# Attention's end taken apart: halves, f32r parts, earlier rows, later ranking

## Chip, cores and metric

One NeuronCore of one Trainium2 chip. The metric is device microseconds of one execution; lower is better. Traced times count from the start of the profiled span. PE is the matmul engine, DVE the vector engine, ACT the scalar engine, POOL the GpSimd engine, and SP the engine that issues the plain DMAs.

## What is computed

Decayed causal attention, then two mixture-of-experts layers. Cut to what matters here:

```python
attn_out = _attn_ref(q, k, v, f)             # 2 batches, 8 heads, 576 positions, head size 64
x = attn_out.transpose(0, 2, 1, 3).reshape(1152, 512)
# layer 1: each token goes to ONE of 8 experts (argmax of x @ w_gate), capacity 288
disp[e, counts[e]] = x[i]                    # slots are given in token order
h = relu(disp @ w1[e]);  y = h @ w2[e]       # 512 -> 1024 -> 512, float32
out[i] = gate_w[i] * y[expert_idx[i], pos[i]]
# layer 2: the two best of 8 experts by noisy logits, weighted, same matrix sizes
```

## The kernel before

**Attention** (`phase_a`) works in nine units of 128 token rows (`ORDER` 0, 1, 2, 3, 4, 6, 7, 8, 9; the last is 9, called `LAST`; unit 0 holds the first rows of both batches). A unit has four head pairs, and a step of the loop over `n` takes one pair through scores, softmax, transposes and the product with V, each stage some steps behind. Work at a unit's end is entered in a table with `at(step, function, unit)`. With n the step of a unit's last product plus one:

- `fin` (line 317) copies the product from PSUM to `xT` on ACT;
- `finx` (line 333) makes, for two head pairs at a time, token rows (`xr`) and gate logits (`lgp`) with float32 matmuls on PE (line 340), which DVE scales (lines 344 and 347);
- `route1` (line 361) finds each token's expert (DVE) and the softmax weight (ACT);
- `route2` (line 389) counts tokens ahead of each token with three small matmuls (`pp`), makes the slot `sl` on DVE and starts a scatter of the rows to `xs` in HBM from POOL (line 426).

The rows of units 8 and 9 come too late to go through HBM for the first expert. `route2` therefore keeps them on chip (`g.late1`) with a one-hot matrix `oh` (line 403). `route2(8)` has SP read the first expert's 192 rows `xg0` from `xs` (line 425), ahead of the scatters of units 8 and 9. `place` (line 434) transposes `xg0` into two PSUM banks `pa` and adds unit 8 as a matmul with its one-hot; `first` (line 874) adds unit 9 (line 884) and splits the sum into f32r high and low parts `X` (lines 887 and 888). The rank of the experts by load (`rank_count`, `rank_order`, lines 675 to 700) is the last thing that attention emits; its order decides which rows and weights SP asks for next.

**Layer 1** (`moe1`): three experts run in f32r with split weights, five in float32. `Weights.split` makes `whi` on ACT (line 760) and `wlo` on DVE (line 768) of a 128x512 weight block. `ffn1(0, f)` multiplies X with block f (lines 844 and 845, three PSUM banks in turn), ACT copies half of the result (`ha`, line 848), DVE adds the other half (`hs`, line 849), ACT applies the relu (`H`, line 852). After `ffn1(0, 0)` and `ffn1(0, 1)` one more block is split, between `hs` and `H`.

**Order.** In attention SP and PE run in the order of the program and the other engines in an order that the framework plans; both layers run in the program's order on every engine. The pools `mp`, `wp` and `wr2` of the layers take the memory of attention's pool `ap`, so their first writer waits until everything that reads or writes an `ap` tile is over, a DMA that reads its slot numbers `sl` included. Two accesses to one PSUM bank of which one writes keep their order too: in `rank_order` the matmul of line 698 writes the bank that the copies of lines 696 and 697 read.

Of the kernel before, what the change touches and what calls it, by code (L numbers as in the profile page):

```python
# [134 lines left out]
def phase_a(g, q, k, v, f, wg, noise, out):  # L135
# [180 lines left out]

    def fin(i):
        b, c = units[i]
        s0, r = (0, P) if i == 0 else CHUNKS[c]
        nmax, rsum, pv = st[i]  # L320
        xT = ap.tile([P, KD, P], F32, tag="xT", name="xT", bufs=2)
        nc.scalar.activation(xT[:, :, :r], pv[:, :, :r], AF.Copy)
# [8 lines left out]
        st[i] = (xT, rinv, xr, lgp)  # L331

    def finx(i, half):
        b, c = units[i]
        s0, r = (0, P) if i == 0 else CHUNKS[c]
        xT, rinv, xr, lgp = st[i]
# [10 lines left out]
        nc.vector.tensor_tensor(  # L347
            xr[:r, h0 * D:(h0 + 4) * D].rearrange("q (j h d) -> q j h d", j=2, h=2), pxv[:, :, :P].rearrange("q j (h d) -> q j h d", h=2),
            rv[:, :, :, None].to_broadcast([r, 2, 2, D]), op=ALU.mult)

# [9 lines left out]

    def route1(i):
        b, c = units[i]
        s0, r = (0, P) if i == 0 else CHUNKS[c]
        xT, rinv, xr, lgp = st[i]
# [4 lines left out]
        lg, mx, gs, ef, lim, ng = s[:r, 0:8], s[:r, 8:16], s[:r, 16:17], s[:r, 17:18], s[:r, 18:19], s[:r, 20:21]  # L369
# [3 lines left out]
        nc.vector.max_index(iu[:r], mx, lg)  # L373
        nc.vector.tensor_copy(ef, iu[:r, 0:1])
# [14 lines left out]
    def route2(i):  # L389
# [10 lines left out]
        if i >= LAST - 1:  # L400
            oh = cp.tile([P, CAP1[0]], F32, tag=f"oh{i}", name="oh0")
            nc.vector.scalar_tensor_tensor(s[:, 22:23], pp[:, 0:1], 1.0, ohb[:, 0:1], op0=ALU.add, op1=ALU.mult)
            nc.vector.tensor_scalar(oh, g.iow[:, :CAP1[0]], s[:, 22:23], None, op0=ALU.is_equal)
            g.late1.append((xr, oh))
        nc.vector.scalar_tensor_tensor(s[m, 32:40], pp[m, :E], 1.0, ohb[m], op0=ALU.mult, op1=ALU.mult, accum_out=pos)
# [27 lines left out]
    def place(h):  # L433
# [4 lines left out]
        for d in (2 * h, 2 * h + 1):  # L438
            for t in range(2):
                nc.tensor.matmul(g.pa1[h][:, d % 2, t * T:(t + 1) * T], g.xg0[:T, t, d * P:(d + 1) * P], g.ident[:T, :T], start=d % 2 == 0 and t == 0, stop=False)  # L440
# [43 lines left out]
    at(first[6] - 8, load_v, 5)  # L484
    for i in ORDER:
        n = last[i] + LAG + 1
        at(n, fin, i)
        n2 = n + 1 if i == LAST else n + 2
        at(n + 1, finx, i, 0)
        at(n2, finx, i, 1)  # L490
        at(n2, route1, i)
        if i == LAST:
            at(n + 1, place, 0)
            at(n + 3, place, 1)
        at(max(n + (2 if i == LAST else 3), 21 + i if i else 0), route2, i)
    at(last[4] + LAG + 5, route2, 5)
    for n in range(len(work) + LAG + 9):
# [23 lines left out]
        if n >= 20:  # L521
            init_step(g, g.init2)
    g.order1.rank(ohs, g.caps[:, 0:E], g.pxx)

# [142 lines left out]
class Order:  # L667
    def __init__(self, g, name):
        self.g, self.name, self.reg, self.perm = g, name, {}, None

    def rank(self, ohs, caps, pool):
        self.rank_count(ohs, pool)
        self.rank_order(caps, pool)

# [112 lines left out]
def moe1(g, x_rows, w1, w2, wg2, wn2):  # L787
# [87 lines left out]
    def first():  # L875
# [4 lines left out]
        X[0] = mp.tile([P, KD, 2 * C], F32R, tag="X", name="X", bufs=1)  # L880
        xr, oh = g.late1[1]
        for d in range(KD):
            pa = g.pa1[d // 2]
            nc.tensor.matmul(pa[:, d % 2, :], xr[:, d * P:(d + 1) * P], oh, start=False, stop=d % 2 == 1)
            if d % 2:
# [361 lines left out]
```

## Time and profile before

| what | us |
|---|---|
| median of 3 runs (lowest, highest) | 572.6 (571.42, 573.81) |
| the profiled execution | 571.73 |
| its span in the trace | 569.9 |
| PE busy in the span | 548.5 |
| DVE busy | 330.8 |
| ACT busy | 257.0 |
| POOL busy | 108.6 |

Times of single instructions come from the profiled execution. Around its span lie 1.8 us; its own time is 0.9 us under the median of the runs. The trace says for each stretch what ran on each engine, what an engine waited for, and the share of full speed that was granted to PE's clock.

### The profile page before, as it was taken

The page shows a single profiled execution, that of the slowest core. Times are in us where ns is not written, and L with a number is a line of the kernel's source. Part 1 is how long each engine was busy: PE and PEld are TensorE (multiplying, and loading weights), DVE is VectorE, ACT ScalarE, POOL GpSimd, SP SyncE. Part 2 cuts the span into 40 slices and gives each one's busy share as a digit, 9 for nine tenths or more (in the row PEclk, how much of TensorE's full clock was granted, in tenths as well). Part 3 has the DMA queues.
Part 4 walks back from the last instruction along what each step waited for, and adds up shares of the span by engine and source line. Part 5 has one row for each costly group of instructions (what it writes and reads, how often), then busy time and mean ns, then how long its engine had stood idle before and what let it go on. Part 6 is the DMA issues. An engine that isn't in the chain of part 4 may idle for free.

```text
span 569.9 us, 11856 instructions
## 1 busy us (share of the span) xinstructions
PE 548.5 (96%) x4288; PEld 505.5 (89%) x4288; DVE 330.8 (58%) x1100; ACT 257.0 (45%) x642; POOL 108.6 (19%) x168
## 2 busy tenths in 40 slices
PE   8999999999999999999998999999999999999994
PEld 4566776677899999999998999999999999999993
DVE  4577767776754542332335765756666666766642
ACT  3656555553556442122125344444454545454520
POOL 4010003100000302202201720130313121224131
PEclk9999999999999999999999999999999999999998
DMA  6988917925499968678777279967586667642021
GB/s 149 241 209 223 290 57 230 374 88 198 112 369 315 319 241 263 215 233 276 239 243 208 69 213 370 288 211 205 177 221 196 218 192 230 192 121 59 23 71 49
DMA packets 103858, 116.80 MB, mean 205 GB/s; under 512 B 38189, under 2 KB 73037, under 8 KB 103792
## 3 DMA queue, kind: packets, MB, share of 16 engines
q1 hardware_dynamic: 97120, 99.86, 59.4%
q0 software_dynamic: 6528, 16.06, 8.3%
q8 instruction: 36, 0.59, 0.5%
q14 instruction: 30, 0.25, 0.1%
q10 hardware_dynamic: 144, 0.04, 0.0%
HBM read 91.63 MB, written 25.85 MB: 206 GB/s over the span
## 4 chain that ended last, share of the span: by engine, by line
PE 81%; DVE 5%; issue 4%; DMA 4%; ACT 3%; SPq 2%; POOL 0%; POOLq 0%; ACTq 0%; DVEq 0%
PE py L1020 19%; PE ps L1009 19%; PE py L858 14%; PE psn L834 7%; PE ps L844 3%; PE pyr L581 3%; PE sc L248 2%; PE pyr L1042 2%; PE pv L315 2%; PE pt L289 2%; DMA kn<-in_k_dram 2%; PE ps L845 1%; PE pt L206 1%; PE pt L978 1%; DVE t L258 1%
## 5 line engine op out<-in xcount | busy, mean ns | idle before, releaser
L768 DVE TENSOR_TENSOR wlo<-wr,whi 128x512 fp32r<-128x512 f32 x152 | 102.9, 689 | 25.4 <-ACT whi L760 22.9
L1009 PE MATMUL ps<-X,whi 128*128 128x312 f32 (+4 forms) x512 | 110.2, 306 | 0.0
L1020 PE MATMUL py<-H,whi 128*128 128x312 f32 (+4 forms) x512 | 109.8, 306 | 0.0
L760 ACT ACTIVATE whi<-wr 128x512 fp32r<-128x512 f32 x152 | 93.0, 625 | 27.5 <-PE py L1020 21.3
L1009 PEld LDWEIGHTS ps<-X,whi 128*128 128x128 f32 x512 | 83.4, 189 | 0.1
L1020 PEld LDWEIGHTS py<-H,whi 128*128 128x128 f32 x512 | 83.4, 188 | 0.0
L858 PE MATMUL py<-H,wr 128*128 128x192 f32 (+7 forms) x512 | 80.9, 314 | 0.0
L1009 PE MATMUL ps<-X,wlo 128*128 128x312 f32 (+4 forms) x256 | 77.4, 302 | 0.0
L1020 PE MATMUL py<-H,wlo 128*128 128x312 f32 (+4 forms) x256 | 77.3, 302 | 0.0
L858 PEld LDWEIGHTS py<-H,wr 128*128 128x128 f32 x512 | 76.0, 190 | 0.8
L638 POOL DMA_INDIRECT x<-yr,sl x30 | 34.4, 1146 | 134.2 <-ACT Xn L820 48.8
L266 ACT ACTIVATE pr<-t,nmax 128x192 f32<-128x192 f32 (+4 forms) x72 | 41.9, 583 | 37.5 <-DVE nmax L258 31.5
L1045 POOL DMA_INDIRECT out_dram<-ot,tk x24 | 27.4, 1140 | 148.2 <-DVE ot L1044 147.8
L1011 ACT ACTIVATE H<-ps 128x312 fp32r<-128x312 f32 (+4 forms) x64 | 27.1, 424 | 61.2 <-PE ps L1009 59.0
L1013 DVE SCALAR_TENSOR_TENSOR H<-ps,H 128x312 fp32r<-128x312 f32 (+4 forms) x64 | 30.4, 474 | 31.3 <-ACT H L1011 30.8
L1009 PEld LDWEIGHTS ps<-X,wlo 128*128 128x128 f32 x256 | 48.2, 188 | 0.0
L1020 PEld LDWEIGHTS py<-H,wlo 128*128 128x128 f32 x256 | 48.1, 188 | 0.0
L834 PE MATMUL psn<-Xn,wr 128*128 128x176 f32 (+4 forms) x320 | 46.3, 295 | 0.0
L834 PEld LDWEIGHTS psn<-Xn,wr 128*128 128x128 f32 x320 | 43.5, 190 | 0.0
L258 DVE CUSTOM_DVE_ANT_0 t<-sc,WB 128x192 f32<-128x192 f32 (+3 forms) x64 | 28.6, 477 | 5.4 <-PE sc L251 3.7
L844 PE MATMUL ps<-X,whi 128*128 128x384 f32 (+2 forms) x96 | 31.4, 383 | 0.3 <-DVE hs L849 0.2
L248 PE MATMUL sc<-kT,qT 64*128 64x288 f32 (+4 forms) x264 | 30.1, 330 | 0.4 <-DVE nmax L258 0.3
(261 smaller groups left out, 805.6 us busy)
## 6 DMA issues: line engine op xcount, KB each, us to landing
wr<-in_moe_w_dram SPq DMA_DIRECT2D x128, 512.0 KB
xs<-z SPq DMA_DIRECT2D x18, 264.0 KB
x<-z SPq DMA_DIRECT2D x16, 258.0 KB
WB<-ncum SPq DMA_DIRECT2D x4, 576.0 KB
out_dram<-z SPq DMA_DIRECT2D x9, 256.0 KB
qn<-in_q_dram SPq DMA_DIRECT2D x8, 256.0 KB
kn<-in_k_dram SPq DMA_DIRECT2D x8, 256.0 KB
x2g<-x SPq DMA_DIRECT2D x3, 628.9 KB
```

Of the source, the lines that this page charges most:

```text
L248: nc.tensor.matmul(ps[hh][:r, :a1 - a0], a[sl, p, :r], bb[sl] if i == 0 else bb[sl, a0:a1], start=m == 0, stop=m == 2 and (i == 0 or a1 < w))
L258: nc.vector.tensor_tensor_reduce(out=ts[hh][:r, a0:a1], in0=ps[hh][:r, :a1 - a0], in1=WB[b][:r, h, a0:a1] if i else Wd[0][:r, h, :r], op0= ...
L266: nc.scalar.activation(dst, src, AF.Exp, bias=nmax[:r, h:h + 1], scale=-1.0, accum_out=rsum[:r, h:h + 1])
L638: d = nc.gpsimd.indirect_dma_start(out=g.x2, out_offset=bass.IndirectOffsetOnAxis(ap=sl[:T, t, kk:kk + 1], axis=0), in_=yr[:T, t], in_offs ...
L760: self.g.nc.scalar.activation(self.hi[u], self.g.stream.view(self.base + u), AF.Copy)
L768: self.g.nc.vector.tensor_tensor(self.lo[u], self.g.stream.view(self.base + u), self.hi[u], op=ALU.subtract)
L834: nc.tensor.matmul(ps[:, :C], w[:, d, :], X[e][:, d, :], start=d == 0, stop=d == KD - 1)
L844: nc.tensor.matmul(ps[:, :2 * C], hi[:, d, :], X[e][:, d, :], start=d == 0, stop=False)
L858: nc.tensor.matmul(py[dd][:, :C], w[:, dd, :], H[e][:, f, :], start=f == 0, stop=f == KF - 1)
L1009: nc.tensor.matmul(ps[:, :C], w[:, d, :], X[e][:, x, d, :], start=d == 0 and i == 0, stop=d == KD - 1 and i == 2)
L1013: nc.vector.scalar_tensor_tensor(H[e][:, 1, f, :], ps[:, :C], 0.0, H[e][:, 0, f, :], op0=ALU.max, op1=ALU.subtract)
L1020: nc.tensor.matmul(py[dd][:, :C], w[:, dd, :], H[e][:, x, f, :], start=f == 0 and i == 0, stop=f == KF - 1 and i == 2)
```

## The change

1. **Last unit in halves.** `fin(9)` is two ACT copies. The first half's copy and `finx(9, 0)` move ahead of the last head pair's product; the second half's `finx` follows `place(0)`. The rows of its second half are scaled by four ACT copies in place of one DVE instruction.
2. **f32r parts.** A new `halves` copies the rows of units 8 and 9 to an f32r high part on ACT and subtracts it on DVE for a low part, 256 columns at a time. The one-hots become f32r, and `place8` and `first` multiply both parts.
3. **First expert's rows.** `early_rows` requests `xg0` in two DMAs three steps before the last unit's end, and `place` no longer holds unit 8. `xg0` and unit 8's parts lie in `ap` slots of the loaded K and Q rows.
4. **Routing in two pieces.** `route1` becomes `route1a` (maximum and its index) and `route1b` (the rest). For units before 8 `route1a` moves one step later, `route1b` two, `route2` two. For unit 8 nothing moves, for unit 9 all follow `place8(1)`.
5. **Ranking.** `rank` at attention's end goes. `rank_count` stands among the first weight splits, `rank_order` after `ffn1(0, 1)`, and with it the requests for the next experts' rows and weights. The two weight blocks that the first expert still lacks are requested before it (limit 8).
6. The slot numbers of unit 8 move from `ap` to the pool that stays (`cp`), as those of unit 9 did.

```diff
-    def fin(i):
+    def fin(i, half=None):
...
+        ps = slice(0, KD) if half is None else slice(2 * half, 2 * half + 2)
+        if half == 1:
+            nc.scalar.activation(st[i, "x"][0][:, ps, :r], pv[:, ps, :r], AF.Copy)
+            return
...
+    def halves(i, half):
+        x = g.late1[i]
...
+        m = slice(256 * half, 256 * half + 256)
+        nc.scalar.activation(x[1][:, m], x[0][:, m], AF.Copy)
+        nc.vector.tensor_tensor(x[2][:, m], x[0][:, m], x[1][:, m], op=ALU.subtract)
...
+        if i == LAST and half == 1:
+            for h in range(4):
+                nc.scalar.activation(xr[:, (h0 + h) * D:(h0 + h + 1) * D], pxv[:, h // 2, h % 2 * D:h % 2 * D + D], AF.Copy, scale=rinv[:, h0 + h:h0 + h + 1])
...
+        if i >= LAST - 1:
+            if half == 0:
+                g.late1.append([xr])
+            if i < LAST or half == 0:
+                halves(i - LAST + 1, half)
...
+        if i == LAST:
+            halves(1, 1)
...
-            oh = cp.tile([P, CAP1[0]], F32, tag=f"oh{i}", name="oh0")
+            oh = cp.tile([P, CAP1[0]], F32R, tag=f"oh{i}", name="oh0")
...
-        elif i == LAST:
-            sl = cp.tile([P, 1], I32, tag="sll", name="sl")
+        elif i >= LAST - 1:
+            sl = cp.tile([P, 1], I32, tag=f"sl{i}", name="sl")
...
-        if i == LAST - 1:
-            g.xg0 = cp.tile([P, 2, DM], F32, tag="xg0", name="xg0")
-            T = CAP1[0] // 2
-            nc.sync.dma_start(g.xg0[:T], g.xs[0:2 * T, :DM].rearrange("(t p) w -> p t w", p=T))
...
+    def early_rows():
+        T = CAP1[0] // 2
+        g.xg0 = [ap.tile([P, DM], F32, tag=t, name="xg0", bufs=2) for t in ("kn", "qn")]
+        for t in range(2):
+            nc.sync.dma_start(g.xg0[t][:T], g.xs[t * T:(t + 1) * T, :DM])
...
-        xr, oh = g.late1[0]
+
+    def place8(h):
+        _, hi, lo, oh = g.late1[0]
         for d in (2 * h, 2 * h + 1):
-            nc.tensor.matmul(g.pa1[h][:, d % 2, :], xr[:, d * P:(d + 1) * P], oh, start=False, stop=False)
+            for x in (hi, lo):
+                nc.tensor.matmul(g.pa1[h][:, d % 2, :], x[:, d * P:(d + 1) * P], oh, start=False, stop=False)
...
+    for i in ORDER[:-1]:
         n = last[i] + LAG + 1
+        m = n + 2 if i == LAST - 1 else n + 3
         at(n, fin, i)
...
+        at(n + 2, finx, i, 1)
+        at(m, route1a, i)
+        at(m if i == LAST - 1 else m + 1, route1b, i)
+        at(max(n + 3 if i == LAST - 1 else n + 5, 21 + i if i else 0), route2, i)
+    n = last[LAST] + LAG + 1
+    at(n - 3, early_rows)
+    at(n - 2, fin, LAST, 0)
+    at(n - 1, finx, LAST, 0)
+    at(n, fin, LAST, 1)
+    at(n, place, 0)
+    at(n + 1, finx, LAST, 1)
+    for fn, a in ((place8, (0,)), (place, (1,)), (place8, (1,)), (route1a, (LAST,)), (route1b, (LAST,)), (route2, (LAST,))):
+        at(n + 1, fn, *a)
...
-    g.order1.rank(ohs, g.caps[:, 0:E], g.pxx)
...
     W.split()
     first()
-    xg[1] = rows(1)
-    xg[2] = rows(2)
-    g.stream.limit = 9 * E
+    g.stream.limit = 8
     g.stream.pump()
-    W.split(5)
+    W.split(2)
+    g.order1.rank_count(g.ohs, g.pxx)
+    W.split(3)
...
             ffn1(e, f)
+            if e == 0 and f == 1:
+                g.order1.rank_order(g.caps[:, 0:E], g.pxx)
+                xg[1] = rows(1)
+                xg[2] = rows(2)
+                g.stream.limit = 9 * E
+                g.stream.pump()
```

## Rows read from the trace of the kernel before

Lengths and starts are in us.

**Rows 1.** The page, part 4: shares of the chain that ended last.

```profile
PE 81%; DVE 5%; issue 4%; DMA 4%; ACT 3%; SPq 2%; POOL 0%; POOLq 0%; ACTq 0%; DVEq 0%
```

**Rows 2.** Stretches: length, busy time (instructions) of PE, PEld, DVE, ACT, POOL; clock, DMA.

```profile
130.00:140.00 10.00, 9.28 (x110) 7.51 (x109) 5.52 (x29) 4.13 (x11) 0.97 (x1) 1.00 0.67 233
160.00:170.00 10.00, 10.00 (x65) 9.86 (x64) 6.57 (x12) 5.86 (x12) 0.00 (x0) 1.00 1.07 367
```

**Rows 3.** Timeline of PE, 139 to 158: start, length, line, tiles, count.

```profile
139.74 1.25 PE L340 MATMUL px<-IW,xT 128*128 128x144 f32 x8 [0.72 <-ACT xT L322]
140.82 1.03 PE L440 MATMUL pa<-ident,xg 96*128 96x96 f32 x8
141.69 0.84 PE L443 MATMUL pa<-oh,xrl 128*128 128x192 f32 x4
144.57 1.24 PE L884 MATMUL pa<-oh,xrl 128*128 128x192 f32 x6
147.48 0.42 PE L844 MATMUL ps<-X,whi 128*128 128x384 f32 x1
150.40 0.36 PE L844 MATMUL ps<-X,whi 128*128 128x384 f32 x1
150.69 0.36 PE L844 MATMUL ps<-X,whi 128*128 128x384 f32 x1
151.64 0.44 PE L844 MATMUL ps<-X,whi 128*128 128x384 f32 x1 [0.22 <-DVE hs L849]
157.45 1.48 PE L858 MATMUL py<-H,wr 128*128 128x192 f32 x8
```

**Rows 4.** Timeline of DVE, 143 to 153, columns as before.

```profile
143.12 0.32 DVE L403 TENSOR_SCALAR oh<-iow,rtl 128x192 f32<-128x192 f32 x1
145.45 0.15 DVE L682 SCALAR_TENSOR_TENSOR rks<-prk,tie 8x8 f32<-8x8 f32 x1
145.96 0.21 DVE L686 SCALAR_TENSOR_TENSOR rks<-io,rks,one 8x8 f32<-8x8 f32 x1
146.81 0.55 DVE L888 TENSOR_TENSOR X<-pa,X 128x384 fp32r<-128x384 f32 x1
147.69 0.56 DVE L888 TENSOR_TENSOR X<-pa,X 128x384 fp32r<-128x384 f32 x1
151.23 0.35 DVE L849 TENSOR_TENSOR hs<-ps,ha 128x192 f32<-128x192 f32 x1
152.75 0.69 DVE L768 TENSOR_TENSOR wlo<-wr,whi 128x512 fp32r<-128x512 f32 x1 [0.16 <-ACT whi L760]
```

**Rows 5.** Source line L760, 142.75 to 142.85: ACT's sequencer.

```profile
L760 ACTq EVENT_SEMAPHORE  x1: 1112/1112/1112, 142.7 to 142.7; - x1
```

**Rows 6.** Timeline of POOL, the scatter of unit 8.

```profile
138.82 0.97 POOL L426 DMA_INDIRECT xs<-xrl,sl  x1 [12.31 <-DMA x<-z]
```

**Rows 7.** Timeline of PE in the second layer's first expert.

```profile
331.21 0.38 PE L698 MATMUL prq<-rks 8*128 8x8 f32 x2 [0.87 <-DVE perm L697]
```

**Rows 8.** Timeline of DVE at the same place.

```profile
330.93 0.16 DVE L696 CAST permi<-prq 128x8 int32<-128x8 f32 x1
```

**Rows 9.** Chain of waits, 110 to 152: start, length, what.

```profile
125.53 3.28 DMA xs<-xr,sl
128.83 0.35 SPq L425
```

**Rows 10.** Waits of PE, 20 to 140: total, times, longest.

```profile
PE pt L206 <- DVE rt L374: 1.5, 2, 0.9
PE px L340 <- DVE rt L405: 0.7, 2, 0.4
PE pt L206 <- DVE rt L416: 0.6, 1, 0.6
```

**Rows 11.** Stretches at the end, columns as in Rows 2.

```profile
562.50:563.00 0.50, 0.20 (x2) 0.00 (x0) 0.36 (x2) 0.00 (x0) 0.50 (x1) 1.00 0.00 0
564.50:565.00 0.50, 0.00 (x0) 0.00 (x0) 0.00 (x0) 0.00 (x0) 0.28 (x1) 0.50 0.08 25
```

More of the change, by code (lines that the diff above doesn't have):

```diff
@@ L315, in pvmm @@
                     nc.tensor.matmul(pv[o, p, :r], vt[b * 5 + j][:, 2 * p + hh, :], sb[:, n, :r], start=False, stop=j == c)
-    def fin(i):
+    def fin(i, half=None):
         b, c = units[i]
         s0, r = (0, P) if i == 0 else CHUNKS[c]
-        nmax, rsum, pv = st[i]
+        nmax, rsum, pv = st[i][:3]
+        ps = slice(0, KD) if half is None else slice(2 * half, 2 * half + 2)
+        if half == 1:
+            nc.scalar.activation(st[i, "x"][0][:, ps, :r], pv[:, ps, :r], AF.Copy)
+            return
         xT = ap.tile([P, KD, P], F32, tag="xT", name="xT", bufs=2)
-        nc.scalar.activation(xT[:, :, :r], pv[:, :, :r], AF.Copy)
+        nc.scalar.activation(xT[:, ps, :r], pv[:, ps, :r], AF.Copy)
         rinv = ap.tile([P, H], F32, tag="rinv", name="rinv", bufs=2)
@@ L330, in fin @@
         lgp = ap.tile([P, H, E], F32, tag="lgp", name="lgp", bufs=2)
-        st[i] = (xT, rinv, xr, lgp)
+        st[i, "x"] = (xT, rinv, xr, lgp)
+    def halves(i, half):
+        x = g.late1[i]
+        if len(x) == 1:
+            x += [ap.tile([P, DM], F32R, tag=t, name=n, bufs=2) if i == 0 else cp.tile([P, DM], F32R, tag=n + "l", name=n) for t, n in (("kn", "xrh"), ("qn", "xrL"))]
+        m = slice(256 * half, 256 * half + 256)
+        nc.scalar.activation(x[1][:, m], x[0][:, m], AF.Copy)
+        nc.vector.tensor_tensor(x[2][:, m], x[0][:, m], x[1][:, m], op=ALU.subtract)
     def finx(i, half):
@@ L335, in finx @@
         s0, r = (0, P) if i == 0 else CHUNKS[c]
-        xT, rinv, xr, lgp = st[i]
+        xT, rinv, xr, lgp = st[i, "x"]
         px = (g.psc if i == LAST else g.pxx).tile([P, 512], "px")
@@ L346, in finx @@
             rv[:, :, :, None].to_broadcast([r, 2, 2, E]), op=ALU.mult)
-        nc.vector.tensor_tensor(
-            xr[:r, h0 * D:(h0 + 4) * D].rearrange("q (j h d) -> q j h d", j=2, h=2), pxv[:, :, :P].rearrange("q j (h d) -> q j h d", h=2),
-            rv[:, :, :, None].to_broadcast([r, 2, 2, D]), op=ALU.mult)
+        if i == LAST and half == 1:
+            for h in range(4):
+                nc.scalar.activation(xr[:, (h0 + h) * D:(h0 + h + 1) * D], pxv[:, h // 2, h % 2 * D:h % 2 * D + D], AF.Copy, scale=rinv[:, h0 + h:h0 + h + 1])
+        else:
+            nc.vector.tensor_tensor(
+                xr[:r, h0 * D:(h0 + 4) * D].rearrange("q (j h d) -> q j h d", j=2, h=2), pxv[:, :, :P].rearrange("q j (h d) -> q j h d", h=2),
+                rv[:, :, :, None].to_broadcast([r, 2, 2, D]), op=ALU.mult)
+        if i >= LAST - 1:
[3 more added lines that the diff above has]
+                halves(i - LAST + 1, half)
     ohs = g.ohs = cp.tile([P, E], BF16, tag="ohs", name="ohs")
@@ L359, in load_noise, with route1a @@
             nc.sync.dma_start(nz[:, 1 + 4 * b:5 + 4 * b], noise[b * S + 64:b * S + S].rearrange("(c p) w -> p c w", p=P))
-    def route1(i):
+    def route1a(i):
         b, c = units[i]
         s0, r = (0, P) if i == 0 else CHUNKS[c]
-        xT, rinv, xr, lgp = st[i]
+        xT, rinv, xr, lgp = st[i, "x"]
         if i == LAST:
@@ L368, in route1 @@
             s = ap.tile([P, 64], F32, tag="rt0" if i == 0 else "rt", name="rt", bufs=1 if i == 0 else 4)
-        lg, mx, gs, ef, lim, ng = s[:r, 0:8], s[:r, 8:16], s[:r, 16:17], s[:r, 17:18], s[:r, 18:19], s[:r, 20:21]
+        lg, mx = s[:r, 0:8], s[:r, 8:16]
         nc.vector.tensor_reduce(lg, lgp[:r].rearrange("p h e -> p e h"), axis=AX.X, op=ALU.add)
@@ L373, in route1, with route1b @@
         nc.vector.max_index(iu[:r], mx, lg)
+        st[i, "r"] = (s, iu)
+    def route1b(i):
+        b, c = units[i]
+        s0, r = (0, P) if i == 0 else CHUNKS[c]
+        xT, rinv, xr, lgp = st.pop((i, "x"))
+        s, iu = st.pop((i, "r"))
+        lg, mx, gs, ef, lim, ng = s[:r, 0:8], s[:r, 8:16], s[:r, 16:17], s[:r, 17:18], s[:r, 18:19], s[:r, 20:21]
         nc.vector.tensor_copy(ef, iu[:r, 0:1])
@@ L400, in route2 @@
         if i >= LAST - 1:
-            oh = cp.tile([P, CAP1[0]], F32, tag=f"oh{i}", name="oh0")
+            oh = cp.tile([P, CAP1[0]], F32R, tag=f"oh{i}", name="oh0")
             nc.vector.scalar_tensor_tensor(s[:, 22:23], pp[:, 0:1], 1.0, ohb[:, 0:1], op0=ALU.add, op1=ALU.mult)
             nc.vector.tensor_scalar(oh, g.iow[:, :CAP1[0]], s[:, 22:23], None, op0=ALU.is_equal)
-            g.late1.append((xr, oh))
+            g.late1[i - LAST + 1].append(oh)
         nc.vector.scalar_tensor_tensor(s[m, 32:40], pp[m, :E], 1.0, ohb[m], op0=ALU.mult, op1=ALU.mult, accum_out=pos)
@@ L439, in place @@
             for t in range(2):
-                nc.tensor.matmul(g.pa1[h][:, d % 2, t * T:(t + 1) * T], g.xg0[:T, t, d * P:(d + 1) * P], g.ident[:T, :T], start=d % 2 == 0 and t == 0, stop=False)
-        xr, oh = g.late1[0]
+                nc.tensor.matmul(g.pa1[h][:, d % 2, t * T:(t + 1) * T], g.xg0[t][:T, d * P:(d + 1) * P], g.ident[:T, :T], start=d % 2 == 0 and t == 0, stop=False)
+    def place8(h):
+        _, hi, lo, oh = g.late1[0]
         for d in (2 * h, 2 * h + 1):
-            nc.tensor.matmul(g.pa1[h][:, d % 2, :], xr[:, d * P:(d + 1) * P], oh, start=False, stop=False)
+            for x in (hi, lo):
+                nc.tensor.matmul(g.pa1[h][:, d % 2, :], x[:, d * P:(d + 1) * P], oh, start=False, stop=False)
     work = [(i, p) for i in ORDER for p in range(KD)]
@@ L484, in phase_a @@
     at(first[6] - 8, load_v, 5)
-    for i in ORDER:
+    for i in ORDER[:-1]:
         n = last[i] + LAG + 1
+        m = n + 2 if i == LAST - 1 else n + 3
         at(n, fin, i)
-        n2 = n + 1 if i == LAST else n + 2
         at(n + 1, finx, i, 0)
[L490 to L496, printed above, removed]
+        at(n + 2, finx, i, 1)
[11 more added lines that the diff above has]
+        at(n + 1, fn, *a)
+    at(last[4] + LAG + 7, route2, 5)
     for n in range(len(work) + LAG + 9):
@@ L669, in __init__ @@
         self.g, self.name, self.reg, self.perm = g, name, {}, None
-    def rank(self, ohs, caps, pool):
-        self.rank_count(ohs, pool)
-        self.rank_order(caps, pool)
     def rank_count(self, ohs, pool):
@@ L880, in first @@
         X[0] = mp.tile([P, KD, 2 * C], F32R, tag="X", name="X", bufs=1)
-        xr, oh = g.late1[1]
+        _, hi, lo, oh = g.late1[1]
         for d in range(KD):
             pa = g.pa1[d // 2]
-            nc.tensor.matmul(pa[:, d % 2, :], xr[:, d * P:(d + 1) * P], oh, start=False, stop=d % 2 == 1)
+            for x in (hi, lo):
+                nc.tensor.matmul(pa[:, d % 2, :], x[:, d * P:(d + 1) * P], oh, start=False, stop=x is lo and d % 2 == 1)
             if d % 2:
```

## The prediction

> **What bounds the kernel now.** I read the page's chain first, then the stretches around attention's end, then the timelines of PE, DVE and ACT there, and last the sequencers' own waits. The chain says that PE's work is 81% of what ended last [rows 1]. From the first expert's second product on PE never pauses (10.00 us busy in 10.00) [rows 2]. So a change at attention's end is worth exactly what it moves the start of that product, `ffn2(0)`, now at 157.45 [rows 3]; nothing behind it absorbs or multiplies the shift. Every term below is a shift of that start.
>
> Between attention's last product and 157.45 PE works almost without a gap, but partly on small float32 matmuls, and the reader is to see what paces them. After the last product PE waits 0.72 for the copy `xT`, makes eight `px` matmuls, eight that transpose `xg0`, four of unit 8's rows, and from 144.57 unit 9's rows; `ffn1` starts at 147.48 [rows 3]. Then DVE paces: the two low parts of X end at 147.36 and 148.25 (146.81 + 0.55, 147.69 + 0.56), late because the ranking stood before them, 145.45 to 146.17; five weight splits follow, and the first `hs` comes at 151.23, 2.98 behind the end of X [rows 4]. The third `ffn1` step could start at 150.40, the fourth waited 0.22 for that `hs` [rows 3]. A second wait is hidden in ACT's sequencer: it stood 1112 ns from 142.7 on one semaphore ahead of the first `whi` [rows 5]. The instruction is one of those that wait for all users of attention's pool, and the one user still open then was unit 8's scatter, begun at 138.82, whose slot numbers lie there [rows 6]. It landed near 143.8, five microseconds after its start.
>
> **The change, part by part.**
>
> *Last unit in halves, f32r parts.* Times are on the clock of before. Four of the eight `px` matmuls go ahead of the last product; eight take 1.08 up to the next line's start (139.74 to 140.82), so four take 0.54 [rows 3]. The product, which ended at 139.0, now ends at 139.55. The copy of half of `xT` runs under `place(0)`, 0.87 (140.82 to 141.69) [rows 3], so PE reaches the second half's `px` at 140.4 and ends it at 140.95, with the last one's pipeline at 141.1. Unit 8's matmuls took 0.84 for four in float32; a 384-column and a 192-column f32r matmul together take 0.29 (150.40 to 150.69) [rows 3], so I take 0.4 for four of 192 columns. `place8(0)`, `place(1)` and `place8(1)` end at 140.95 + 0.4 + 0.87 + 0.4 = 142.6. The routing chain from the last `px` (end 140.99) to the end of the one-hot (143.12 + 0.32) took 2.45 before [rows 3, 4]; less about 0.3, since scaling the rows leaves DVE for ACT, it ends at 141.1 + 2.15 = 143.25. I take 143.5, for PE's small matmuls queue behind `place8(1)`. Unit 9's matmuls, 0.4 with 0.25 of pipeline for the first bank, give 144.15; ACT's copy 0.49 as an estimate from the X parts beside it (0.55 [rows 4]), DVE's low parts 0.55 each: they end at about 145.25 and 145.85. `ffn1` starts at 145.35 instead of 147.48. The `whi` before it is no bar: the scatter of unit 8 leaves its list, because `sl` moves to `cp`, and PE's last use of the pool ends at 142.6. The second low part, which starts the count of the next step, comes 2.4 earlier (148.25 to 145.85). Bounds 1.7 to 3.0, by how the planned engines order the extra copies. Those are three copies on ACT and three subtractions on DVE before the product ends, each about half of a 0.69 weight split [rows 4]; DVE is busy 5.52 of 10 there and ACT 4.13 [rows 2], which hides them. If that cover failed, they would cost up to 3 x 0.35 = 1.0.
>
> *Ranking later.* Its two pieces go into orders that are fixed. `rank_count` takes 0.72 on DVE (145.45 to 145.96 + 0.21) [rows 4] and stands between the second and third of the five splits, so the first `hs` comes 2.98 + 0.75 behind X: 145.85 + 3.75 = 149.6. That alone would still be a gain. But `rank_order` now stands on PE between the second and the third `ffn1` step, and its second matmul (L698) must wait until DVE has copied `permi` and `perm` out of the same bank. On DVE these copies stand behind both `hs` and the two splits between them. From the first `hs` to the end of the last split took 2.2 (151.23 to 152.75 + 0.69) [rows 4]; copies and semaphore add 0.3 (330.93 to 331.21) [rows 7, 8]. So L698 starts at 149.6 + 2.2 + 0.3 = 152.1 and the third step at 152.4, in place of 150.40. Queued behind L698 on PE is everything: steps three to eight. They now run unbroken, six times 1.16 (151.64 to 157.45 is five of them [rows 3]), 7.0, and `ffn2(0)` starts at 159.4. Net of the 2.4 that X gained, that is +1.9. The second layer has the same construction, and its L698 did wait, 0.87 [rows 7]; here DVE's queue is longer, so PE stands some four microseconds, from about 148 to 152.1. Bounds +1.2 to +2.6.
>
> SP's requests move too. Rows 1 and 2 and the later weights follow `permi`, some five microseconds later than now; their first use follows the second product's start. The two blocks that the first expert lacks are asked for before the ranking. I cost this at nothing.
>
> *First rows sooner.* SP reads `xs` only when unit 7's scatter has landed, 3.28 behind its start at 125.53, and the request went out at once, at 128.83 [rows 9]: SP stood waiting there, so a place earlier in the program buys nothing. Yet `route2(7)` moves two steps later. Between the scatters of units 7 and 8 lie four steps of the loop (125.53 to 138.82 [rows 6, 9]), 3.3 each, so unit 7's now starts near 132.2 and lands near 135.5. With 0.35 for each of two requests [rows 9], and as an estimate the scatter's own 3.28 for the data, `xg0` is there near 139.5, just as `place(0)` wants it at 139.55. I take +0.2, bounds 0 and +1.5, the latter if DVE gets to that slot a microsecond later.
>
> *Routing in two pieces.* In attention PE waited behind DVE's routing instructions 1.5 + 0.7 + 0.6 = 2.8 [rows 10]. Maximum, the rest and the slots now fall into three steps. I take -1.0, nearer to a third of it than to all, because the waits are for copies that only queue among the routing; bounds -2.8 and +1.0 (the cover above).
>
> *PE's clock.* A standing PE can lose its full clock. At the trace's end the granted clock was still 1.00 in the half microsecond in which the last matmul ended, and 0.50, the lower of the two levels (1.2 GHz), from 564.50 on, 1.8 behind it [rows 11]. A pause of four is longer. No row shows matmuls at the lower level. The bounds are nothing, if the level comes back with the work, and 7.0, if all six remaining steps run at half speed. I take +2.0, nearly two of the six steps doubled, nearer the low end because PE is busy without a break from then on.
>
> The Trainium skill (TensorE: Matmul & The Clock Gate, "What's actually happening") speaks against this change: "the default state is throttled, and activity releases the throttle". By that the pause costs the clock and the work gives it back; the trace agrees with the first half at its end, and no run here yet shows the second.
>
> **The sum.** -1.0 + 0.2 + 1.9 + 2.0 = +3.1. On the profiled execution's own 571.73 (span 569.9 and 1.8 around it) that gives 574.8; the median of the runs, 572.6, lies 0.9 above that execution, so I predict 575.7.
>
> **The rivals.**
>
> *The clock stays up.* The same stall, but the pause is broken by two tiny matmuls of `rank_order` at its start and may be too short: 1.1 more than before, 573.7. For it: the second layer's pause of 0.87 left the clock alone. Against it: four is not 0.87.
>
> *Faster: L698 doesn't stand.* If the copies of `permi` and `perm` reach DVE ahead of the second `hs`, or PE's third step may pass L698, only the `hs` of 149.6 bars the fourth step; it ends at 149.95, and five steps bring `ffn2(0)` to 155.8, -1.65. With -1.0 and +0.2 that is -2.4: 570.2. It decides from the point where L698's wait is under some two microseconds. Against it: rows 7 and 8 show this very wait where the order is made the same way.
>
> *The change does not bring the rows sooner.* If unit 7's slot is late on DVE, `place(0)` stands up to 1.5 and with it the second half's `px`; and if splitting the routing gains nothing, the sum is 0 + 1.5 + 1.9 + 2.0 = +5.4: 578.0.
>
> **How the numbers follow.** The forecast (stall and lower clock) gets 0.45, with a range of its own from 573.8 to 578.5; the clock that stays up 0.25; no stall 0.18; late rows 0.12. Half a percent of 572.6, 2.9, is about what a measurement of this kernel can tell from no change: the lines are 569.7 and 575.5. Slower by more: two thirds of the forecast's chance, all of the late rows, a little of the second case, 0.44. Faster by more: the faster rival with the whole 2.8 of the routing waits, 0.10. Between: 0.46. The range for eight in ten runs from 570.2, the faster rival, to 578.5.
>
> **What would show it.** Right: in the changed kernel PE's idle time ahead of L698 at about 148 to 152, put down to `perm`, some 3.5 to 4; a granted clock of 0.5 in a stretch right behind it; `ffn1` starting some two microseconds nearer to attention's last product; the long semaphore ahead of the first `whi` gone; `xg0` requested after 135, not before 128.8. Wrong: an L698 wait under 2, or a clock of 1.00 through the stall, or a wait of PE on `xg0` of more than 1. What would break the whole sum is a pause behind `ffn2(0)`, if the later requests for rows and weights reach PE.

## The result and the profile after

| | before | after |
|---|---|---|
| median (lowest, highest; runs) | 572.01 (570.87, 573.81; 4 runs) | 581.22 (577.99, 582.49; 4 runs) |
| ratio, 95% interval | | 1.0134 [1.0105, 1.0162] |
| profiled execution, its span | 571.73, 569.9 | 577.99, 576.2 |
| attention's last row of products (`pvmm`) starts | 137.92 | 141.89 |
| first `ffn1` starts | 147.48 | 149.28 |
| `ffn2(0)` starts | 157.45 | 164.48 |
| first `xsplit` of expert 1 starts | 158.78 | 166.54 |
| from there to the end of the span | 411.1 | 409.7 |

The change is 1.3% slower by the ratio on record (the two medians of the table by themselves give 1.6%); predicted were 575.7 and at most 578.5. `xsplit` is the transposing of an expert's rows on PE, for which the rows must have come from HBM. In the two profiles the loss is +6.3: `ffn2(0)` 7.03 later, 0.73 more up to the first `xsplit`, and 1.4 given back behind it (a wait of PE of 1.3, `pyr` for `l`, that of these two profiles only before's has; why, no run shows).

Timelines of before that these starts rest on: PE, then SP (what it sends), then POOL, whose first use of expert 1's rows had waited for them:

```profile
137.92 1.09 PE L315 MATMUL pv<-PT,v 128*64 128x128 f32 x16
...
158.78 0.57 PE L816 MATMUL pt<-ident,xg 120*128 120x120 f32 x4
```

```profile
128.83 0.35 SPq L425 DMA_DIRECT2D xg<-xs  x1
129.22 9.25 SPq L545 DMA_DIRECT2D x<-z  x10
...
149.94 1.51 SPq L801 DMA_DIRECT2D xg<-xs  x2
```

```profile
154.88 0.20 POOL L819 COPY xm<-xg 120x20 f32<-120x20 f32 x1 [8.10 <-DMA xg<-xs]
```

Chain of waits of after, its shares; [rows 1] was 81% PE:

```profile
PE 46%; issue 29%; DMA 8%; POOL 6%; DVE 5%; POOLq 2%; ACT 1%; SPq 1%; DVEq 0%; ACTq 0%
```

The 29% of "issue" are time in which the engine waited for nothing that the profile shows, so the two chains cannot be set against each other step by step.

Waits of PE in attention, after (20 to 145: total, times, longest); they answer to [rows 10]:

```profile
PE pt L206 <- DVE PT L295: 1.9, 3, 1.2
...
PE pp L428 <- DVE xr L363: 1.3, 1, 1.3
...
PE px L352 <- DVE rinv L328: 1.1, 3, 0.4
PE px L352 <- DVE rt L436: 1.0, 3, 0.4
```

The waits behind routing instructions that the change was to remove (`rt` of lines 374 and 416) are gone. New are one of `pp` for `xr`, which is the scaling of the next unit's `px`, and three of `px` for `rinv`. `px` does not read `rinv`; these waits stand right behind a `pp` and end some 0.15 us after DVE's read of that `pp` (line 436), as the waits for `rt` of line 436 end with the read itself: `px` and `pp` wait for each other's readers. Together the three lines are 3.4, where before had 0.7 (`rt` of line 405).

Timeline of PE, after (start, length, line, tiles, count, wait):

```profile
104.92 0.66 PE L352 MATMUL px<-IW,xT 128*128 128x144 f32 x4
106.82 0.19 PE L428 MATMUL pp<-base,ones 1*64 1x8 bf16 x1 [1.25 <-DVE xr L363]
...
141.89 1.10 PE L315 MATMUL pv<-PT,v 128*64 128x128 f32 x16
...
147.37 0.36 PE L923 MATMUL pa<-oh,xrh 128*128 128x192 f32 x1 [0.80 <-DVE oh L434]
...
149.28 0.66 PE L882 MATMUL ps<-X,whi 128*128 128x384 f32 x1 [0.65 <-issue]
...
153.16 0.38 PE L731 MATMUL prq<-rks,eid 8*128 8x8 f32 x2
155.65 0.47 PE L736 MATMUL prq<-rks 8*128 8x8 f32 x2 [2.11 <-DVE perm L735]
156.05 0.69 PE L882 MATMUL ps<-X,whi 128*128 128x384 f32 x1
...
164.48 1.49 PE L896 MATMUL py<-H,wr 128*128 128x192 f32 x8
166.54 0.63 PE L854 MATMUL pt<-ident,xg 120*128 120x120 f32 x4 [0.58 <-DMA xg<-xs]
```

The first pair is the new wait at its place: `px` of the next unit, then `pp` of unit 5, which stands until DVE has read `px`. Line 736 is the old line 698, and it stands for `perm`, as forecast. The last row is the one I had not priced: a PE wait for expert 1's rows.

Stretches of after, PE only (length, busy time and instructions, granted clock, DMA share, GB/s):

```profile
148.00:150.00 2.00, 1.35 (x10) 0.75 0.81 286
150.00:152.00 2.00, 2.00 (x9) 0.50 0.42 156
152.00:154.00 2.00, 1.54 (x10) 0.90 0.89 335
154.00:156.00 2.00, 0.35 (x2) 0.95 0.38 79
156.00:158.00 2.00, 2.00 (x8) 0.50 0.62 74
158.00:160.00 2.00, 2.00 (x11) 0.70 1.02 252
160.00:162.00 2.00, 2.00 (x16) 1.00 0.98 351
```

The clock falls to its lower level (1.2 GHz) twice, and both times comes back while PE works.

Timeline of SP, after (start, length, line, transfer, count); it answers to [rows 9]:

```profile
105.90 0.74 SPq L587 DMA_DIRECT2D x<-z  x1
138.89 0.81 SPq L464 DMA_DIRECT2D xg<-xs  x2
...
140.69 11.92 SPq L587 DMA_DIRECT2D x<-z  x11
...
157.13 1.39 SPq L587 DMA_DIRECT2D x<-z  x3
160.04 2.15 SPq L839 DMA_DIRECT2D xg<-xs  x2
```

SP sends nothing from 106.64 to 138.89. Then it empties, in order, what had queued behind the waiting request of `xg0`: fifteen zero fills of the second layer's table `x` (258 or 137 KB each, some 3.3 MB; one of them is not shown, and the last three are layer 1's own), gate columns and weights, and only then, at 160.04, the rows of experts 1 and 2. Before, that request went out at 149.94.

### The profile page after: what moved, and what is told of

The parts are those of the page before. It is cut to its first block, busy times and chain, and to the rows that moved or that the text cites. A ratio compares the mean times of both kernels' runs of the same rounds, so it can differ in the third digit from the quotient of the medians.

```text
span 576.2 us, 11875 instructions
## 1 busy us (share of the span) xinstructions
PE 551.2 (96%) x4288; PEld 508.2 (88%) x4288; DVE 332.4 (58%) x1103; ACT 260.2 (45%) x651; POOL 107.6 (19%) x168
## 4 chain that ended last, share of the span: by engine, by line
PE 46%; issue 29%; DMA 8%; POOL 6%; DVE 5%; POOLq 2%; ACT 1%; SPq 1%; DVEq 0%; ACTq 0%
PE py L896 13%; PE psn L872 7%; DMA out_dram<-ot,tk 6%; PE sc L248 4%; POOL out_dram L1090 3%; PE pv L315 3%; PE ps L882 3%; PE pt L289 3%; PE pyr L623 2%; PE px L352 2%; POOLq L1123 2%; POOL pv L1040 2%; PE pv L310 2%; PE pt L206 2%; DMA kn<-in_k_dram 1%
## 5 line engine op out<-in xcount | busy, mean ns | idle before, releaser
L882 PE MATMUL ps<-X,whi 128*128 128x384 f32 (+2 forms) x96 | 34.2, 409 | 0.7 <-issue 0.7
```

What stands on the lines that cost most here:

```text
L882: nc.tensor.matmul(ps[:, :2 * C], hi[:, d, :], X[e][:, d, :], start=d == 0, stop=False)
```

## The experiments

Each ratio is to the kernel before, run beside it on the same chip. All kernels compute the whole reference.

### One bank for two things

`pp` and `px` both come from `g.pxx`, a pool of one bank of PSUM, the memory that the matmuls write. Two runs take the collision away in two ways. First, the routing's steps as before, with everything else of the change kept:

```diff
-        m = n + 2 if i == LAST - 1 else n + 3
+        m = n + 2
-        at(m if i == LAST - 1 else m + 1, route1b, i)
+        at(m, route1b, i)
-        at(max(n + 3 if i == LAST - 1 else n + 5, 21 + i if i else 0), route2, i)
+        at(max(n + 3, 21 + i if i else 0), route2, i)
-    at(last[4] + LAG + 7, route2, 5)
+    at(last[4] + LAG + 5, route2, 5)
```

> The changed kernel with the steps of routing as before (route1a and route1b two steps behind fin, route2 three, unit 5's as before); the rest of the change stays. Theory 1, the later steps put the slot matmuls pp beside the next unit's px, which share one PSUM bank: attention's last product ends near 139.7 (before 139.0, changed 143.0), the waits of PE for DVE at pp and px go, and the time falls by 3 to 4 us against the changed kernel, to about 577 (median). Rival, the extra work on ACT and DVE (halves, row scaling) lengthens attention: the last product still ends at 142 or later and the time stays within 1 us of the changed kernel's 581.

Measured 577.0 (575.59 to 578.04), ratio 1.0059 [1.0034, 1.0084]. Second, the new steps, with `pp` in another pool:

```diff
-        pp = g.pxx.tile([P, 512], "pp")
+        pp = g.psc.tile([P, 512], "pp")
```

> The changed kernel with its later routing steps, but pp takes one of the three banks of the scores instead of the one bank that px uses. Theory 1 (the shared bank): PE's waits at pp and px go, the last product ends within 1 us of 139.7, the time falls by about 3 us. Rival (DVE's queue is simply longer in these steps): PE's waits move to the transposes that need DVE's copies, the last product ends after 141.5 and the time falls by less than 1 us.

Measured 578.7 (575.09 to 579.91), ratio 1.0087 [1.0052, 1.0122]. Timeline of PE, the last row of products; first of the run with the steps put back, then of the one with `pp` elsewhere:

```profile
138.76 1.09 PE L315 MATMUL pv<-PT,v 128*64 128x128 f32 x16
```

```profile
137.38 1.09 PE L315 MATMUL pv<-PT,v 128*64 128x128 f32 x16
...
151.14 0.59 PE L736 MATMUL prq<-rks 8*128 8x8 f32 x2 [3.55 <-DVE perm L735]
160.62 1.48 PE L896 MATMUL py<-H,wr 128*128 128x192 f32 x8
```

Either edit alone brings attention back (141.89 in after), and neither profile has a wait of `pp` for `xr` or of `px` for `rinv`; with `pp` elsewhere those for `rt` of line 436 are gone as well. Profiles of one and the same attention differ, too: with after's, the last row starts between 141.13 and 141.89 in four of them (144.36 in a fifth), so most of a microsecond between two profiles is not to be read. The shift here is 3 to 4.5. So it is neither the new steps nor the bank, but both together: two steps later, `pp` of a unit falls into the step in which the next unit's `px` uses the bank. With the bank apart the last row starts 0.54 before its place in the kernel before, although four `px` matmuls now stand ahead of it. But of 4.5 won in attention only 3.86 reach `ffn2(0)`. Line 736 starts 13.76 behind the last row in both kernels; in the second it has stood longer by then (3.55 for 2.11), and from there to `ffn2(0)` it takes 9.48 in place of 8.83, at a granted clock of 0.50 from 150 to 156.

Is the bank a cost in the kernel before too? The same one line there:

> The kernel before with one line changed: `pp` taken from the pool `psc` instead of the single bank of `pxx`. Theory (the bank was a cost in the kernel before too: its waits on routing were 1.5, 0.7 and 0.6 us): last product 1 to 2.8 us earlier than 139.0, time 570.5 to 572.5 against 573.4. Rival (those waits only stood in front of other work): within 0.5 us of the kernel before, 573 to 574.

Measured 574.74 (570.97 to 576.37) against 574.18, ratio 1.0007 [0.9977, 1.0037]: the rival, or just above its range. Without the later steps no gain shows.

### The ranking's stall

The two products of `rank_order` are sent back to back, so that the second no longer waits for the copies of `permi` and `perm`:

```diff
         nc.tensor.matmul(pq[:, 0:E], self.g.eid.to_broadcast([E, P]), oh, start=True, stop=True)
+        if self.name == "1":
+            nc.tensor.matmul(pq[:, E:2 * E], cc.to_broadcast([E, P]), oh, start=True, stop=True)
...
-        nc.tensor.matmul(pq[:, E:2 * E], cc.to_broadcast([E, P]), oh, start=True, stop=True)
+        if self.name != "1":
+            nc.tensor.matmul(pq[:, E:2 * E], cc.to_broadcast([E, P]), oh, start=True, stop=True)
```

> The changed kernel, but in the first layer's rank_order both matmuls stand ahead of DVE's copies, so the second waits for no copy. Theory 2 (PE's stand of 2.1 us at it, and the lower clock behind it, cost the product's start): the gap between the second and third ffn1 steps falls from 2.8 to about 0.5, the second stretch at the lower clock goes, a wait of some 0.5 to 1.5 for hs comes at the fourth step in its place; the second product starts 2.5 to 3.5 us sooner relative to attention's end; time down by about 3 us. Rival (the wait is only put off: hs bars the fourth step by as much): less than 1 us.

Measured 582.67 (582.32 to 585.04), ratio 1.0177 [1.014, 1.0213]. Its timeline of PE:

```profile
158.76 1.48 PE L899 MATMUL py<-H,wr 128*128 128x192 f32 x8
167.87 1.06 PE L857 MATMUL pt<-ident,xg 120*128 120x120 f32 x4 [7.63 <-DMA xg<-xs]
168.72 5.36 PE L899 MATMUL py<-H,wr 128*128 128x192 f32 x24
```

The stall goes, `ffn2(0)` starts 5.7 earlier (5.0 counted from attention's last row, at 141.13 here), and all of it is handed to the next wait: expert 1's rows, asked for at 160.36. Behind that wait the same 24 matmuls take 5.36 in place of 4.07, with a granted clock of 0.50 from 166 to 170. In after, the stall had only stood in front of the rows. The 3 us that I expected did not come.

The other way to try the clock alone: constant matmuls in the three pauses (unit 9's one-hot, X, the ranking), no wait removed:

```diff
+        if self.name == "1":
+            warm(self.g, 10, self.g.ptr)
```

(and the same with 3 and 4 matmuls in the two pauses ahead of it).

> The changed kernel with matmuls on constants (128x512 bf16, results unused) in the three pauses of PE: four ahead of unit 9's rows, three behind them, ten between the two matmuls of rank_order. Theory 3 (the pauses take the clock, and the clock's length at the lower level is what differs from run to run): the granted clock stays 1.00 from 140 to 170, the six steps behind the stall take 7.0 instead of 8.4, the time falls by 1.5 to 4 us and the executions lie closer together than 578 to 582.5. Rival (the clock falls for another reason, or its fall is hidden): the time stays within 0.5 us or rises by the fillers' length, up to 1 us.

Measured 585.86 (583.48 to 586.92), ratio 1.0225 [1.0193, 1.0256]. That is 4.6 over after, and neither what I expected nor the rival. The clock is 1.00 in every stretch from 148 to 166, `ffn2(0)` starts 1.2 earlier than in after, at 163.26 (1.5 counted from attention's last row), and then PE waits 3.81 for the same rows. They were asked for at 160.59 and used from 168.55, 2.0 later than in after; why they landed later, no run shows. So the lower clock was no bound by itself either.

### The queue behind a waiting request

The unsent fills go into SP's queue ahead of `xg0`'s request:

```diff
     def early_rows():
+        while g.init2:
+            init_step(g, g.init2)
         T = CAP1[0] // 2
```

> Only this is changed in the changed kernel: the zero fills of the second table that are still unsent are put into SP's queue ahead of the request of `xg0` instead of behind it (SP stands without work from 106.65 to 138.89 there). Theory A (SP's queue, 3 MB of fills behind a waiting request, sets when expert 1's rows are asked for): the fills go out before 128, the rows are requested at 156.5 to 158 instead of 160.04 (then the ranking at 155.4 is what ends last) and land by 162; the second product still starts at about 164.5, since the ranking's stall on TensorE stays, the wait at the first `xsplit` is 0, and the runs give 576 to 578.5 with less spread. Rival B (SP's queue is only a bystander; the rows land 6 us after any request because of the weights): rows land at 163 or later and the time stays at 579 to 582. Rival C (fills beside the attention's own transfers delay it): last product later than 143.0 by over 0.5, time over 582.

Measured 578.21 (576.96 to 579.64), ratio 1.0096 [1.0058, 1.0133], with after itself beside it:

> The changed kernel itself, once more, beside the next three on one chip. Expected 578 to 582.5, as its first four runs gave. What is asked is where the profiled execution's wait at the first `xsplit` of expert 1 stands: 0.58 us in the profile of after. If the landing of expert 1's rows is what ends last in this kernel, an execution near 581 shows a wait of 2 to 4 us there (or in the second `xsplit`), with a lower granted clock right behind it; if the spread has another origin, the wait is under 1 us and the excess stands elsewhere.

After again: 581.44 (579.06 to 582.08), 1.013 [1.0088, 1.0173]. Its profiled execution, 581.97, waits 1.94 at that `xsplit` in place of 0.58. But 2.5 of its excess of 4.0 over the first profile arises before 30 us, where the granted clock was 0.66 from 20 to 30 (1.00 in the first); that stands ahead of all that the change touches.

Timeline of SP with the fills ahead:

```profile
107.11 21.72 SPq L589 DMA_DIRECT2D x<-z  x19
138.79 0.81 SPq L466 DMA_DIRECT2D xg<-xs  x2
...
155.92 1.55 SPq L841 DMA_DIRECT2D xg<-xs  x2
```

The fills are out by 128.83, in time in which SP sent nothing; attention isn't delayed; the rows are asked for 4.1 earlier and are there 4.7 later, at 160.59 (POOL's first use), and the wait is gone, as theory A had it. Then the two edits together, fills ahead and the ranking's products back to back:

> The ranking's two products sent back to back (which alone gave 582.7 with a wait of 7.63 us for expert 1's rows, though the second product started at 158.76) and the fills ahead of `xg0`'s request. Theory A: the rows are requested at 156 to 158 and land at 160.5 to 163, the wait at the first `xsplit` falls from 7.63 to 0.5 to 3 us, time 575.5 to 578.5: what the ranking's stall cost becomes visible only now. Rival B (rows land late by themselves): wait of 6 us or more, 581 to 583.

Measured 573.5 (572.09 to 578.09), ratio 0.9995 [0.9962, 1.0029]. Timeline of PE:

```profile
159.25 1.48 PE L901 MATMUL py<-H,wr 128*128 128x192 f32 x8
160.66 0.63 PE L859 MATMUL pt<-ident,xg 120*128 120x120 f32 x4
```

No wait of these matmuls, where I expected 0.5 to 3, and a time under the expected 575.5. The rows came just in time: the weight load of line 859 stood 0.2 for them. The ratio of after, 1.013, becomes 1.0096 with one edit alone, 1.0177 with the other, and 0.9995 with both. That is how two bounds in parallel show: a stall on PE and a late transfer, each hiding the other.

### All three, and what the parts are worth then

Fills ahead, products back to back, `pp` in the other pool:

> As the one before, and `pp` taken from the other PSUM pool as well. The theory that the three costs (the shared bank in attention, the ranking's stall with its lower clock, the rows behind the fills) are all there is: last product of attention ends at 138.5, second product starts at 154 to 155 (157.45 before), rows requested at 151.5 to 153.5, landed by 156 to 158.5, wait at the first `xsplit` 0 to 2.5, time 570 to 573.5, at or below the kernel before (573.5 on this chip). Rival: if the rows or the clock find another bound, the second product starts at 155 but the time stays over 575.

Measured 569.68 (568.22 to 572.59), ratio 0.9927 [0.9898, 0.9956]: faster than both kernels, and a little under the expected 570. Its profile caught the longest of its eight executions, and there `ffn2(0)` starts only at 159.89. Timeline of PE, and stretches as above, of that profile:

```profile
139.71 1.47 PE L475 MATMUL pa<-ident,xg 96*128 96x96 f32 x8 [1.66 <-DMA xg<-xs]
```

```profile
138.00:140.00 2.00, 0.34 (x4) 1.00 0.82 233
140.00:142.00 2.00, 1.90 (x16) 0.93 0.67 225
142.00:144.00 2.00, 2.00 (x11) 0.50 0.67 153
144.00:148.00 4.00, 3.35 (x18) 0.50 0.00 0
148.00:152.00 4.00, 3.76 (x14) 0.51 0.20 69
152.00:154.00 2.00, 2.00 (x15) 1.00 0.70 225
```

In this execution `xg0` is late, 1.66, and the lower clock that follows costs more than the wait: from the last row of products to `ffn2(0)` it took 22.93, against 17.62 in the run before. But the wait is not the kernel's rule. Here the request went out 6.0 after the start of unit 7's scatter (131.16), for which it stands. In the run with the ranking first, below, attention is the same and its last row as early (137.13); the scatter starts at 131.34, the request goes out 3.2 later, and `place(0)` does not wait. Timeline of SP, first of this profile, then of that one:

```profile
137.15 0.88 SPq L466 DMA_DIRECT2D xg<-xs  x2
```

```profile
134.54 0.81 SPq L466 DMA_DIRECT2D xg<-xs  x2
```

With the routing's steps put back as well, unit 7's scatter starts some 6 earlier, and `xg0` should be in time even so:

> The kernel with the fills ahead, `pp` in the other pool and the ranking's products back to back (569.7 in the runs, with a wait of 1.66 us at the first `place` for `xg0` and a lower clock over 140 to 152 behind it), with the routing's steps put back to those of the kernel before. Theory: unit 7's rows are scattered near 126 again, `xg0` is requested near 129, the wait of 1.66 goes, attention's last product stays at 138 to 138.7, the clock stays up over 140 to 152, and the runs give 566.5 to 569.5. Rival: the later steps had their own gain in attention (the routing's DVE work apart from the transposes' copies), so that the last product comes at 139.5 or later and the time is 569.5 to 571.5.

Measured 570.13 (569.57 to 574.48), ratio 0.9954 [0.9927, 0.9981]. Timeline of PE:

```profile
138.01 1.10 PE L315 MATMUL pv<-PT,v 128*64 128x128 f32 x16
145.40 0.41 PE L887 MATMUL ps<-X,whi 128*128 128x384 f32 x1 [0.65 <-issue]
155.63 1.48 PE L901 MATMUL py<-H,wr 128*128 128x192 f32 x8
```

`xg0` is requested at 130.86 (I expected 129), its wait is gone and the clock stays at 1.00, as expected; the median is just above the expected 566.5 to 569.5, in the range of the rival, whose late last row did not come. Whether early or late steps are better the two intervals don't tell apart.

The ranking put back to attention's end, and with it the requests for the next experts' rows and weights, everything else as in the 569.68 kernel:

> The kernel with the fills ahead, `pp` in the other pool and the products back to back, with the ranking at attention's end and the request of expert 1's and 2's rows ahead of the first product, as in the kernel before. It asks what `expert ranking later` is worth by itself. Theory (my prediction's step, 8.46 us from the last product to the first of the expert before and 6.3 after): the first product of the expert starts 1.5 to 2.2 us later, the rows are asked for 6 us earlier but nobody waits for them, time 571 to 572.2 against 569.7. Rival (DVE's queue ends last either way): second product at the same place, 569.5 to 570.3.

Measured 571.88 (570.22 to 575.89), ratio 0.9973 [0.9946, 1.0001], in the expected range: ranking later is worth some 2 us, once neither its stall nor the fills stand in the way; the two intervals just overlap. The profiles agree: from the last row to `ffn2(0)` it takes 19.72 with the ranking first and 17.62 with it later and the steps put back. In the kernel before it took 19.53. So halves and f32r parts show no gain on this way while the ranking stands first; the clock was 0.76 there from 144 to 148 (1.00 in before), and no run takes them out singly. The fills ahead in the kernel before:

> The kernel before with the zero fills ahead of `xg0`'s request, and nothing else. There the request waits only until 128.83 and the rows are asked for at 149.94, after the copy of `xm` at 148.84. Theory (the fills cost only where what stands behind them binds, and here it doesn't): the same time, 572.5 to 574.3. Rival (the fills also hold weights that the first product needs): faster by 1 us or more, under 572.3.

Measured 572.27 (571.01 to 574.07), ratio 0.9969 [0.9939, 0.9999]. That is under the theory's range by 0.2 and inside the rival's (under 572.3), 1.9 under the 574.18 beside it, with an interval that ends just below 1. Its profile gives the rival no support: rows asked for at 148.90 and `ffn2(0)` at 156.84 are 1.0 and 0.6 earlier than in before's profile, but the kernel before with the other bank, which was no faster, has 149.31 and 156.82. So it stays open; a gain of some tenths of a per cent is not excluded. And the request of `xg0` went out at 131.70 in place of 128.83: from the start of unit 7's scatter to that request it took 6.3, as in the two profiles above (6.0 and 5.8), against 3.0 to 3.6 in the eleven others. In these three the last fill had gone out at most 2.1 before the scatter began, in the other runs with fills ahead at least 5.6 before. That fills still under way draw out the scatter fits this, but no run tries it alone.

## Why the prediction was wrong

The sum, term by term, as shifts of `ffn2(0)`:

| step | predicted | measured |
|---|---|---|
| routing in two pieces | -1.0 (-2.8 to +1.0) | +3.43 |
| first rows sooner | +0.2 (0 to +1.5) | 0 |
| halves, f32r, ranking later | +1.9 (+1.2 to +2.6) | +2.1 |
| PE's clock | +2.0 (0 to +7.0) | +1.5 |
| sum | +3.1 | +7.0 |
| later requests for rows and weights | 0 | +0.73, and the bound behind all others |

**Routing in two pieces** is the step that failed in the sum. The last row of products starts 3.97 later, of which 0.54 are the planned `px` matmuls: +3.43, past the upper end of my bounds. With the steps put back it starts at 138.76, so 3.1 of it go with the steps. I had priced the waits that go, and as the upper end DVE's cover; I did not ask with what `route2` would share its new step. The front says that two accesses to one bank keep their order, and I applied that to the ranking only, not to `pp` and `px`. The gain I had taken is real: with `pp` elsewhere the last row starts at 137.38, less 0.54 is 136.84, 1.08 before the 137.92 of the kernel before, where I had -1.0; that it is so near is luck, by the spread between profiles. The Trainium skill (Perfetto Trace Analysis, "Matmuls") has the rule: "Independent matmul groups should rotate through different PSUM banks so the ACT/DVE evacuation of one overlaps the next group's matmuls". After and the run with `pp` elsewhere agree with it, with 4.5 us between one bank and two; with the old steps the second bank won nothing that shows (ratio 1.0007).

**Later requests for rows and weights** is the second step that failed, and the graver one: "their first use follows the second product's start", and "I cost this at nothing", though the prediction's last sentence names it as what would break the sum. In the kernel before there was slack: asked for at 149.94 and landed 4.9 later, at 154.88, the rows were there 4 us ahead of their use at 158.78. Five microseconds later, as I had it for the ranking, with their use 3.1 later, they would still have cost nothing. They came 10.1 later (149.94 to 160.04). The reason stands in [rows 9]: the request of `xg0` waits for unit 7's scatter. I used it to show that an earlier place in the program buys nothing. I did not follow what queues behind the waiting request while the scatter moves: the fills, 13.7 of the 21.2 us that SP took up to the rows (138.89 to 160.04). The request came 10.1 later too (128.83 to 138.89): two steps of the loop, which I had, and the 3.4 of attention, which I hadn't. In after the rows cost little to the eye, 0.58; take the stall away and they cost 7.63.

**Halves, f32r, ranking later** was right in mechanism and size. From attention's last row to line 736 I had 13.6 (the product's end at 139.55 less 1.09, to 152.1); it took 13.76 (141.89 to 155.65). The long semaphore of [rows 5] is gone, the longest of that line is 38 ns. The stall itself was 2.1 in place of "some four", barely over the 2 that I had named as a sign against it, since the two `ffn1` steps before it ran at the lower clock and filled 0.96 of it (149.28 to 153.16, against 147.48 to 150.40 in [rows 3]). DVE's queue, not the clock, set the start of line 736 either way, as forecast: it lies 13.76 behind the last row with the clock down ahead of it (after), with the steps put back, with `pp` elsewhere (where the stand is 3.55) and with the clock held at 1.00.

**PE's clock**: the six steps behind the stall took 8.43 (156.05 to 164.48) in place of 6.95 at full clock, +1.5 for +2.0; constant matmuls that hold the clock take 1.5 off, too. The first fall, from 149, I had not foreseen; it cost nothing here. The Trainium skill (TensorE: Matmul & The Clock Gate, "What's actually happening") has the work give the clock back, and the runs now agree with that half too: 0.50 from 156 to 158 and 1.00 from 160, PE busy throughout.

**First rows**: `xg0` was requested at 138.89 where 135.5 was forecast, the difference being attention's own 3.4, and `place(0)` did not wait for it: right. The rival of late rows had the right word and the wrong rows: not the first expert's, but the second's.

**Behind `ffn2(0)`.** That "nothing behind it absorbs or multiplies the shift" rested on one stretch of 10 us. The profile of before has waits of PE of 1.3, 0.9 and 0.7 behind it, and 1.4 of the shift was absorbed there: the profiles lie 6.3 apart, not 7.8.

**The median.** Between the profiled executions I had +3.1 and they show +6.3; between the medians it is +9.2. After's first profile is the fastest of its four runs. Its repetition adds 1.4 for a longer wait at the same `xsplit`, and 2.5 of lower clock at the start. How often the kernel before has that, no profile here shows.

## What to carry to other kernels

When work moves to another step, list what else in that step uses its PSUM bank, and price the readers of that as a wait. When a queue that runs in order takes a request that waits, everything behind it waits as long: put what depends on nothing ahead of it, as two lines did here, and early enough to be out of the way of what the queue waits for (this last half is argued, not shown). And a transfer of which PE's first use lies one matmul group behind the point you compute is not free: price its landing beside PE's path, for the larger of the two decides, and mending one shows nothing until the other is mended.

## What the hardware showed

In the profile of the run with all three edits, behind a wait of PE of 1.66 us, the granted clock went to 0.50 and stayed there from 142 to about 152, though PE was busy 3.35 of 4 and 3.76 of 4 us in the last two of these stretches; from 152 it was 1.00. Constant matmuls that held it at 1.00 in after moved `ffn2(0)` by 1.2 only. And the time a DMA takes from request to landing depended on what had been queued ahead: expert 1's rows landed 4.6 to 4.9 after their request with the fills long out (149.94 to 154.88 in before, 155.92 to 160.59 with the fills ahead, by POOL's first use), and 6.5 to 8.0 in kernels that had just sent them (160.04 to 166.5 by the chain of after; 160.36 to 167.87, where PE started on them, with the products back to back; 160.59 to 168.55 with the constant matmuls). The edit that sends the fills first changes nothing else, and takes 6.5 to 4.7.
